# Pooled attention scores on the four free tiles of TensorE's array, between the local scores

## Chip, core and metric

The kernel runs on one core of one Trainium2 chip. The metric is the device time of one execution in microseconds; the time before is the median of three runs. A core has five engines with queues of their own: TensorE (PE in the profile, with PEld for its weight loads), VectorE (DVE), ScalarE (ACT), GpSimd (POOL) and SyncE (SP), which only issues transfers.

## The reference

An attention with two branches, added, and a gated feed-forward network behind it.

```python
# q, k, v: 8 batches x 8 heads x 576 x 64
q_d = q.reshape(B, H, Sd, factor, D).mean(axis=3)      # factor 4, Sd = 144; k_d, v_d alike
out_d = sm_attn(q_d, k_d, v_d)                         # softmax attention on the pooled sequence
out_up = np.repeat(out_d, factor, axis=2)
mask = np.abs(pos[:, None] - pos[None, :]) < factor    # local branch: 7 keys for each query
scores = np.where(mask, scale * np.matmul(q, k.transpose(0, 1, 3, 2)), -1000000000.0)
out_local = np.matmul(softmax(scores), v)
x = (out_up + out_local).transpose(0, 2, 1, 3).reshape(B * S, H * D)     # 4608 x 512
gate = np.maximum(x @ w_gate, 0.0)                     # 512 x 1536
return (gate * (x @ w_val) @ w_out).astype(np.float32) # 1536 x 512
```

## The kernel before

Two heads of one batch are a pair p, so there are 32 pairs. `pair(p)` builds the steps of one: loading and casting q and k, transposing them (on TensorE for p < 8, by a DMA after that), pooling (`pl`, the reduction at L1507 on VectorE for p >= 4), the scores, both softmaxes, and the products with v, which `xa` adds into the transposed input xT of the network. `first` builds the two first products of the network (L1794) with their ReLU and product on ScalarE and VectorE (L1808, L1815), `second` the last product (L1860) and the output. A planner (`list_schedule`) gives every step a time on its engine from durations and ranks that are written into the kernel, and the program issues them in that order: on each engine the order is fixed, and only semaphores hold an instruction back.

The scores are one TensorE step `S{p}` for p >= 4 (28 steps), made by `emit_S` from `emit_Sl` and then `emit_Sd`, in two PSUM banks. For the first four pairs (`hd`) `Sl{p}` and `Sd{p}` are steps of their own. The two heads lie in the two halves of the partitions, so each matmul takes 64 rows of the array (row half hh). The output is in groups of 32 partitions, and a matmul with 32 weight columns takes one column group c of four. The array is thus used as eight tiles, 2 row halves x 4 column groups.

- *Local scores* (L1519): 12 rounds of four matmuls, each 32 queries against 32 keys. Round i has blocks 2i and 2i + 1 (par = 0, 1) for both heads, on tiles (hh, c = 2 par + hh): (0,0), (1,1), (0,2), (1,3).
- *Pooled scores* (L1538): 3 rounds of four matmuls, 32 pooled queries against all 144 pooled keys, on tiles (hh, c = 2 hh + par): (0,0), (1,2), (0,1), (1,3). They read qkd, which `pl` writes.

Below, L0 to L11 are the local rounds and P0 to P2 the pooled ones. VectorE adds the mask to the local scores (`msk`, L1576) and takes the pooled scores' maximum (`dmx`, L1588); ScalarE takes the pooled exponentials from the other bank (L1601). The pooled weights wd are turned round by TensorE and evicted by `evw` for p < 8, and by a DMA for the others; `wcols(hh, kc)` picks a head's columns of the result, wT, for the product with the pooled v (L1735).

Of the kernel before, what the change touches and what calls it, by code (L numbers as in the profile page):

```python
# [1192 lines left out]
def _sap(t_ap, lo, n, extra_off, free_dims):  # L1193
    pitch = t_ap.ap[0][0]
    return bass.AP(
        tensor=t_ap.tensor,
        offset=t_ap.offset + lo * pitch + extra_off,
        ap=[[pitch, n]] + [list(d) for d in free_dims],
    )
# [22 lines left out]
def kernel(  # L1222
# [10 lines left out]
    nc = tc.nc  # L1233
    B, H, S, D = q.shape
    NP = B * H // 2
    SD = S // 4
# [35 lines left out]
    def many(n, shape, dt, name):  # L1272
        return [pool.tile(shape, dt, name=f"{name}{i}") for i in range(n)]
# [9 lines left out]
    mask_sb = pool.tile([128, 12, 32], BF16, name="mask_sb")  # L1283
    ident = pool.tile([128, 128], FP16, name="ident_sb")
# [11 lines left out]
    wT = many(3, [128, 6, 128], FP16, "wT")  # L1296
    tq = many(3, [128, 9, 128], FP16, "tq")
    sums_sb = pool.tile([128, 256], FP16, name="sums_sb")
    qkd = many(3, [128, 2 * SD], FP16, "qkd")
# [9 lines left out]
    bank = [psum.tile([128, 512], FP32, name=f"bank{i}") for i in range(8)]  # L1309
# [3 lines left out]
    def add(*a, **kw):  # L1313
        o = Op(*a, **kw)
        ops.append(o)
        return o
# [9 lines left out]
    def copies(dst, src, *engines):  # L1326
        def on(eng):
            if eng == ACT:
                return lambda o: nc.scalar.copy(out=dst, in_=src(o))  # L1329
            return lambda o: engine[eng].tensor_copy(out=dst, in_=src(o))  # L1330
        return [(e, d, on(e)) for e, d in engines]

    def add_any(forms, deps, **kw):

        kw.setdefault("bias", 0.8 if kw["prio"] < 200.0 else BIAS)
        return add(*forms[0], deps, alts=forms[1:], **kw)

    def half(i):
        return bank[i].bitcast(FP16)
# [58 lines left out]
    def pair(p):  # L1398
        b, kk = p // 4, p % 4
        base = 2 * p * HS  # L1400
        S4, S3, S2 = p % 4, p % 3, p % 2
# [3 lines left out]
        hd = p < HEAD  # L1405
# [15 lines left out]
        g = p // 2  # L1421
# [43 lines left out]
        step, q0, k0 = (1, 0, S) if p < TD else (2, QK0, QK0 + 1)  # L1465
        qk_sums = _sap(qk_, 0, 128, q0, [[k0 - q0, 2], [4 * step, SD], [step, 4]])

        def cols(hh, t0, n):
            return _sap(qk_, 64 * hh, 64, t0, [[step, n]])

        old_qk = [b3.get("S"), b3.get("pl"), z_qk[S3]]
        if p < TD:
# [4 lines left out]
            for i, t0, nt in ((0, 0, nb0), (1, nb0, tk - nb0)):  # L1477
# [3 lines left out]
                    lambda o, i=i, nt=nt: _sap(half(T.banks[i]), 0, 128, 0,  # L1481
                                               [[1, 2], [2, nj], [n2, nt]]),
# [27 lines left out]
            pl = add(DVE, 1.35, emit_pool, [*evs, b3.get("S")], prio=P + 14, name=f"pl{p}")  # L1510
        r["pl"] = pl

        def local_scores(scv):
            for i in range(12):
                for par in range(2):
                    blk = 2 * i + par
                    for hh in range(2):
                        c = 2 * par + hh
                        nc.tensor.matmul(  # L1519
                            out=scv[32 * c : 32 * c + 32, i, :],  # L1520
                            lhsT=cols(hh, q0 + step * 24 * blk, 32),
                            rhs=cols(hh, k0 + step * (24 * blk - 3), 32),
                            start=not hd, stop=not hd or i == 11)

        def emit_Sl(o):
            if hd:
                nc.tensor.matmul(out=bank[o.banks[0]][:, 0:384], lhsT=ident, rhs=mask_sb,
                                 start=True, stop=False)
            local_scores(bank[o.banks[0]][:, 0:384].rearrange("p (i j) -> p i j", j=32))

        def emit_Sd(o):
            spv = bank[o.banks[-1]][:, 0 : 3 * SD].rearrange("p (i j) -> p i j", j=SD)
            for i in range(3):
                for par in range(2):
                    g = 2 * i + par
                    for hh in range(2):
                        c = 2 * hh + par
                        nc.tensor.matmul(  # L1538
                            out=spv[32 * c : 32 * c + 32, i, :],
                            lhsT=qkd[S3][64 * hh : 64 * hh + 64, 24 * g : 24 * g + 32],  # L1540
                            rhs=qkd[S3][64 * hh : 64 * hh + 64, SD : 2 * SD],
                            start=True, stop=True)

        def emit_S(o):
            emit_Sl(o)
            emit_Sd(o)
        if hd:
            Sx = add(PE, 0.65, emit_Sl, [*evs, ld_mask], prio=P + 20, need=(pool_, 1),
                     key=("S", p), name=f"Sl{p}", n=49)
            r["S"] = Sd = add(PE, 0.45, emit_Sd, [pl, Sx], prio=P + 20.5, need=(pool_, 1),  # L1550
                              key=("Sd", p), name=f"Sd{p}", n=12)
        else:
            r["S"] = Sx = Sd = add(PE, 0.67, emit_S, [*evs, pl], prio=P + 20, need=(pool_, 2),
                                   key=("S", p), name=f"S{p}", n=60, bias=MARGIN)
        kd = Sd.key

        def lview():
            return bank[Sx.banks[0]][:, 0:384].rearrange("p (i j) -> p i j", j=32)

        def dview():  # L1560
            return bank[Sd.banks[-1]][:, 0 : 3 * SD].rearrange("p (i j) -> p i j", j=SD)
# [3 lines left out]
        def bc12(t):  # L1565
            return _sap(t, 0, 128, 0, [[1, 12], [0, 32]])

        if hd:
            mxo = add(DVE, 0.55, lambda o: nc.vector.tensor_reduce(
                out=mx[S3], in_=lview(), axis=AX.X, op=ALU.max), [Sx, z_w], prio=P + 23,  # L1570
                name=f"mx{p}")
            sub = add(DVE, 0.56, lambda o: nc.vector.tensor_tensor(
                out=s_, in0=lview(), in1=bc12(mx[S3]), op=ALU.subtract),
                [mxo, b2.get("exp")], prio=P + 24, free=[("S", p)], name=f"sub{p}")
        else:
            msk = add(DVE, 0.56, lambda o: nc.vector.tensor_tensor(  # L1576
                out=s_, in0=lview(), in1=mask_sb, op=ALU.add),
                [Sx, ld_mask, b2.get("exp")], prio=P + 21, free=[("S", p)], name=f"msk{p}")
            mxo = add(DVE, 0.55, lambda o: nc.vector.tensor_reduce(  # L1579
                out=mx[S3], in_=s_, axis=AX.X, op=ALU.max), [msk, z_w], prio=P + 23,  # L1580
                name=f"mx{p}")
            sub = add_any(either(lambda o, e: e.tensor_tensor(  # L1582
                out=s_, in0=s_, in1=bc12(mx[S3]), op=ALU.subtract), (POOL, 0.84), (DVE, 0.56)),
                [mxo], prio=P + 24, name=f"sub{p}", port=(DVE, POOL))
        r["exp"] = ex = add(ACT, 0.53, lambda o: nc.scalar.activation(
            out=e_, in_=s_, func=AF.Exp, scale=scale),
            [sub, b3.get("tr0"), b3.get("tr1")], prio=P + 25, name=f"exp{p}")
        dmax = add(DVE, 0.60, lambda o: nc.vector.tensor_reduce(  # L1588
            out=nmx[S3][:, 0:3], in_=dview(), axis=AX.X, op=ALU.max,
            negate=True), [Sd, b3.get("nrd")], prio=P + 22, name=f"dmx{p}")  # L1590
        nb = add(POOL, 0.23, lambda o: nc.gpsimd.tensor_scalar(  # L1591
            out=nmb[S3][:, 0:3], in0=nmx[S3][:, 0:3], scalar1=scale / 16.0, scalar2=None,
# [3 lines left out]
        K0, KR = (0, 96) if p < VPOOL else (V0, V0 + 72)  # L1596
# [3 lines left out]
        for i in range(3):  # L1600
            exd.append(add(ACT, 0.37, lambda o, i=i: nc.scalar.activation(  # L1601
                out=_sap(wd_, 0, 128, 256 * i + K0, kd_cols),
# [5 lines left out]
            out=sm[S3], in_=e_, axis=AX.X, op=ALU.add), [ex, warm], prio=P + 26, name=f"sm{p}")  # L1608
# [3 lines left out]
            out=e_, in0=e_, in1=bc12(rs[S3]), op=ALU.mult), (POOL, 0.84), (DVE, 0.5)),  # L1612
            [rco], prio=P + 28, name=f"nrm{p}", port=(DVE, POOL))
        tr = []
        for par in range(2):
            lo = 64 * par
            tr.append(add(DVE, 0.575, lambda o, lo=lo: nc.vector.transpose(  # L1617
                out=at2[S3][lo : lo + 64, :, lo // 2 : lo // 2 + 32],
# [5 lines left out]
            out=rsd[S3].rearrange("p (i k) -> p i k", k=2),  # L1624
# [3 lines left out]
            out=_sap(wd_, 0, 128, K0, w3), in0=_sap(wd_, 0, 128, K0, w3),  # L1628
# [9 lines left out]
        if p < TD:  # L1638
            r["W"] = W = add(PE, 0.34, emit_W, [nrd], prio=P + 30, need=(pool_, 1),
                             key=("W", p), name=f"W{p}", n=6)  # L1640

            evw = add_any(copies(
                _sap(wT[S3], 0, KR, 0, [[48, 6], [2 * SD, 2], [24, 2], [1, 24]]),
                lambda o: _sap(half(W.banks[0]), 0, KR, 0,
                               [[128, 6], [64, 2], [32, 2], [1, 24]]),
                (ACT, 0.64), (DVE, 0.74)),
                [W, b3.get("V")], prio=P + 31, free=[("W", p)], name=f"evw{p}")
            wcols = lambda hh, kc: _sap(wT[S3], 0, KR, (2 * hh + kc) * SD, [[1, SD]])
        else:
            r["W"] = evw = add(SP, 1.5, lambda o: nc.sync.dma_start(  # L1650
                wT[S3], _sap(wd_, 0, 128, 0, [[1, 768]]), transpose=True),
                [nrd, b3.get("V")], prio=P + 30, xfer=0.8, name=f"dW{p}")
            wcols = lambda hh, kc: _sap(wT[S3], 0, KR, 128 * kc + 64 * hh,
                                        [[256, 3], [32, 2], [1, 24]])
        r["evw"] = evw


# [3 lines left out]
        for par in range(2):  # L1661
            for hh in range(2):
                c = 2 * par + hh
# [38 lines left out]
        else:  # L1702
# [8 lines left out]
            else:  # L1711
                l4 = b1["l4"]
            r["vs"] = vso = add_any(either(lambda o, e: e.tensor_tensor(  # L1713
                out=vs[0], in0=v4_[:, :, 0:128], in1=v4_[:, :, 128:256], op=ALU.add),
# [4 lines left out]
                out=vdz4, in0=vs4[:, :, :, 0:64], in1=vs4[:, :, :, 64:128], op=ALU.add),  # L1719
# [5 lines left out]
        def emit_V(o):  # L1725
# [21 lines left out]
            out=od_sb[S2], in_=bank[V.banks[0]][:, 288 : 288 + SD], mul=0.25),  # L1747
# [212 lines left out]
```

## Time and profile before

| | |
|---|---|
| time, median of 3 runs (lowest to highest) | 364.08 us (363.34 to 364.46) |
| the profiled execution: its span, from the first to the last instruction | 365.8 us |
| mean clock granted to TensorE | 0.991 |
| local score matmuls, L1519: number, busy, mean | 1536, 16.9 us, 177 ns |
| pooled score matmuls, L1538: number, busy, mean | 384, 12.0 us, 225 ns |

The span is taken from one profiled execution; its own time is that span, 0.5% over the median of the runs, which were taken without a profile. Times in the profile are in us unless marked ns. A matmul's record has a start and a modelled end; matmuls overlap, so busy times of TensorE are not added up from means. In a row of busy time by stretch, each engine has its busy time and, behind an x, how many of its instructions ran in the stretch; then come TensorE's granted clock, the share of the DMA engines, and GB/s. In a row of waits stand the waiting engine with its line, what released it, the time in all, how often, and the longest.

### The profile page before, as it was taken

What the parts mean: (1) busy time and instruction counts of PE and PEld (TensorE: products, weight loads), DVE (VectorE), ACT (ScalarE), POOL (GpSimd) and SP (SyncE); (2) the same over time, 40 slices, a digit from 0 to 9 for tenths busy, and PEclk for the clock granted to TensorE, in tenths of its full rate; (3) what the DMA queues carried; (4) which work ended last, traced back from release to release, by engine and by line L of the source; (5) the groups of instructions that cost most, each with busy time, mean ns of one, the idle gap of its engine ahead of it and who ended that gap; (6) DMA issues with size and microseconds to landing.
All of it is one profiled execution on the core that took longest, in us unless ns stands there. A gap on an engine that the chain in (4) does not pass through costs nothing.

```text
span 365.8 us, 10503 instructions
## 1 busy us (share of the span) xinstructions
PE 354.5 (97%) x4241; PEld 183.5 (50%) x4241; DVE 248.5 (68%) x477; ACT 203.0 (55%) x481; POOL 204.7 (56%) x240
## 2 busy tenths in 40 slices
PE   8869999999999999999999999999999999999996
PEld 3536556445554554545454445544545554445554
DVE  4557789726889698887895986788988853322210
ACT  2356977536875667556566675768565433223222
POOL 7677575861557979675888458585799400000000
PEclk9979999999999999999999999999999999999999
DMA  7999999489999999999999999999996121011012
GB/s 189 161 246 274 196 222 300 82 150 192 235 233 219 257 263 148 250 200 273 230 182 238 185 293 160 200 269 211 229 236 109 25 80 57 0 59 57 1 68 107
DMA packets 122067, 64.80 MB, mean 177 GB/s; under 512 B 100386, under 2 KB 106402, under 8 KB 122018
## 3 DMA queue, kind: packets, MB, share of 16 engines
q1 hardware_dynamic: 116194, 59.41, 75.2%
q0 software_dynamic: 5824, 4.72, 8.4%
q8 instruction: 33, 0.54, 0.6%
q14 instruction: 16, 0.13, 0.1%
HBM read 47.59 MB, written 9.44 MB: 156 GB/s over the span
## 4 chain that ended last, share of the span: by engine, by line
PE 90%; DMA 4%; DVE 2%; SPq 1%; POOL 1%; issue 1%; ACT 1%; POOLq 0%
PE bank L1794 52%; PE bank L1860 25%; PE bank L1519 4%; PE bank L1727 2%; DMA gT<-in_k_dram 2%; PE bank L1735 2%; DMA mask_sb<-band_mask 2%; PE bank L1538 2%; PE bank L1636 1%; PE bank L1691 1%; PE bank L1456 1%; DVE vw L1352 1%; PE bank L1839 1%; SPq L1430 1%; SPq L1676 1%
## 5 line engine op out<-in xcount | busy, mean ns | idle before, releaser
L1815 DVE TENSOR_TENSOR gT<-r,bank 128x512 f16<-128x512 f16 (+1 forms) x112 | 74.6, 667 | 64.3 <-PE bank L1794 61.2
L1794 PE MATMUL bank<-xT,wv_sb 128*128 128x512 f16 (+2 forms) x528 | 112.4, 341 | 0.1
L1794 PE MATMUL bank<-xT,wg_sb 128*128 128x512 f16 (+2 forms) x528 | 112.2, 341 | 0.0
L1808 ACT ACTIVATE r<-bank 128x512 f16<-128x512 f32 (+1 forms) x112 | 65.1, 582 | 70.0 <-PE bank L1794 62.9
L1860 PE MATMUL bank<-wo_sb,gT 128*128 128x512 f16 x420 | 96.6, 379 | 0.0
L1794 PEld LDWEIGHTS <-wg_sb 128*128 128x128 f16 x528 | 44.2, 98 | 46.5 <-issue 0.6
L1794 PEld LDWEIGHTS <-wv_sb 128*128 128x128 f16 x528 | 44.2, 98 | 45.5 <-issue 1.0
L1860 PEld LDWEIGHTS <-gT 128*128 128x128 f16 x420 | 39.8, 98 | 45.2 <-issue 0.4
L1869 ACT COPY y_sb<-bank 128x512 f32<-128x512 f32 x35 | 20.5, 586 | 51.5 <-PE bank L1860 51.5
L1330 POOL CAST vw<-vw 128x1536 f16<-128x1536 f32 x28 | 40.9, 1462 | 4.0 <-PE bank L1860 2.3
L1507 DVE TENSOR_REDUCE qkd<-qkT 128x288 f16<-128x1152 f16 x28 | 37.6, 1342 | 3.5 <-ACT qkT L1329 3.1
L1601 ACT ACTIVATE wd<-bank,nmb 128x144 f16<-128x144 f32 x96 | 35.6, 380 | 6.3 <-POOL nmb L1591 5.5
L1582 POOL TENSOR_TENSOR s_sb<-s_sb,mx 128x384 f32<-128x384 f32 x28 | 23.3, 832 | 27.0 <-DVE mx L1579 26.8
L1617 DVE STREAM_TRANSPOSE at<-e 64x384 f16<-64x384 f16 x64 | 36.4, 569 | 2.0 <-POOL e L1611 1.3
L1611 POOL TENSOR_TENSOR e<-e,rs 128x384 f16<-128x384 f16 x32 | 26.8, 839 | 15.1 <-DVE rs L1609 11.8
L1627 POOL TENSOR_TENSOR wd<-wd,rsd 128x432 f16<-128x432 f16 x32 | 29.0, 909 | 9.3 <-DVE rsd L1623 7.6
L1755 DVE TENSOR_TENSOR xT<-bank,od_sb 128x288 f16<-128x288 f32 (+2 forms) x68 | 26.7, 431 | 10.0 <-ACT od_sb L1746 9.8
L1329 ACT COPY qkT<-tq 128x1152 f16<-128x1152 f16 x21 | 25.3, 1204 | 3.0 <-DMA tq<-c 3.0
L1713 POOL TENSOR_TENSOR vs<-v 104x512 f32<-104x512 f32 x20 | 25.4, 1269 | 0.9 <-DMA v<-in_v_dram 0.6
L1330 POOL CAST c<-qk 128x1152 f16<-128x1152 f32 x16 | 18.2, 1147 | 5.5 <-issue 3.2
L1588 DVE TENSOR_REDUCE nmx<-bank 128x3 f32<-128x432 f32 x32 | 19.0, 594 | 3.2 <-PE bank L1538 3.1
L1519 PEld LDWEIGHTS <-qkT 64*32 64x32 f16 x1536 | 13.8, 90 | 12.9 <-issue 7.2
(67 smaller groups left out, 349.9 us busy)
## 6 DMA issues: line engine op xcount, KB each, us to landing
vw<-in_v_dram SPq DMA_DIRECT2D x126, 96.0 KB, 4.8
out_dram<-y_sb SPq DMA_DIRECT2D x16, 512.0 KB, 3.4
qk<-in_q_dram SPq DMA_DIRECT2D x14, 576.0 KB, 6.7
qk<-in_k_dram SPq DMA_DIRECT2D x14, 576.0 KB, 6.4
v<-in_v_dram SPq DMA_DIRECT2D x10, 640.0 KB, 6.5
wv_sb<-in_moe_w_val_dram POOLq DMA_DIRECT2D x4, 384.0 KB, 9.3
wg_sb<-in_moe_w_gate_dram POOLq DMA_DIRECT2D x4, 384.0 KB, 9.4
wo_sb<-in_moe_w_out_dram POOLq DMA_DIRECT2D x4, 384.0 KB, 7.2
```

The source lines that it names most:

```text
L1330: return lambda o: engine[eng].tensor_copy(out=dst, in_=src(o))
L1507: nc.vector.tensor_reduce(out=qkd[S3].rearrange("p (x t) -> p x t", x=2), in_=qk_sums, axis=AX.X, op=ALU.add)
L1519: nc.tensor.matmul(out=scv[32 * c : 32 * c + 32, i, :], lhsT=cols(hh, q0 + step * 24 * blk, 32), rhs=cols(hh, k0 + step * (24 * blk - 3), 32),
L1601: exd.append(add(ACT, 0.37, lambda o, i=i: nc.scalar.activation(out=_sap(wd_, 0, 128, 256 * i + K0, kd_cols), in_=_sap(dview()[:, i, :], 0 ...
L1611: r["nrm"] = nrm = add_any(either(lambda o, e: e.tensor_tensor(out=e_, in0=e_, in1=bc12(rs[S3]), op=ALU.mult), (POOL, 0.84), (DVE, 0.5)), ...
L1617: tr.append(add(DVE, 0.575, lambda o, lo=lo: nc.vector.transpose(out=at2[S3][lo : lo + 64, :, lo // 2 : lo // 2 + 32], in_=e_[lo : lo + 64 ...
L1627: r["nrd"] = nrd = add_any(either(lambda o, e: e.tensor_tensor(out=_sap(wd_, 0, 128, K0, w3), in0=_sap(wd_, 0, 128, K0, w3), in1=_sap(rsd[ ...
L1755: nc.vector.tensor_tensor(out=xT[:, kk, (c1 + lo) % XR : (c1 + lo) % XR + hi - lo].rearrange("p (t f) -> p t f", f=4), in0=bank[V.banks[hf ...
L1794: nc.tensor.matmul(out=bank[(h or o).banks[0]][:, n * x : n * x + n], lhsT=w_sb[:, kk, bass.ts(jj, 128)], rhs=xT[:, kk, x_col(t0) : x_col( ...
L1808: rl = add(ACT, 0.17 + 0.00083 * n * m, lambda o: nc.scalar.activation(out=rt[:, 0 : n * m], in_=bank[f1.banks[0]][:, 0 : n * m], func=AF. ...
L1815: gm = add(DVE, 0.15 + 0.00104 * n * m, lambda o: nc.vector.tensor_tensor(out=gT[:, js[0] : js[0] + m, pos : pos + n], in0=rt[:, 0 : n * m ...
L1860: nc.tensor.matmul(out=bank[parts[0].banks[0]], lhsT=gT[:, jj, col : col + 128], rhs=wo_sb[:, jj, :], start=(jj == 0), stop=(jj == NJJ - 1))
```

## The change

The local and the pooled loops become functions of one round, `local_round` and `pooled_round`. `emit_S` issues a pooled round behind local rounds 0, 2 and 4. The pooled matmuls move to other column groups: c = 2 par + 1 - hh, that is tiles (0,1), (1,0), (0,3), (1,2), the four that a local round leaves free. With that the 32-partition groups of the pooled scores hold other head and block combinations, so `evw` reads them in another order and `wcols` takes other columns. The steps, their durations in the planner, and the order of steps on every engine stay.

```diff
-        def local_scores(scv):
+        def local_round(scv, i):
+            for par in range(2):
+                blk = 2 * i + par
+                for hh in range(2):
+                    c = 2 * par + hh
...
+        def pooled_round(spv, i):
+            for par in range(2):
+                g = 2 * i + par
+                for hh in range(2):
+                    c = 2 * par + 1 - hh
+                    nc.tensor.matmul(
+                        out=spv[32 * c : 32 * c + 32, i, :],
+                        lhsT=qkd[S3][64 * hh : 64 * hh + 64, 24 * g : 24 * g + 32],
+                        rhs=qkd[S3][64 * hh : 64 * hh + 64, SD : 2 * SD],
+                        start=True, stop=True)
...
         def emit_Sd(o):
-            spv = bank[o.banks[-1]][:, 0 : 3 * SD].rearrange("p (i j) -> p i j", j=SD)
             for i in range(3):
-                for par in range(2):
-                    g = 2 * i + par
-                    for hh in range(2):
-                        c = 2 * hh + par
...
+                pooled_round(dview(), i)
 
         def emit_S(o):
-            emit_Sl(o)
-            emit_Sd(o)
+            for i in range(12):
+                local_round(lview(), i)
+                if i % 2 == 0 and i < 6:
+                    pooled_round(dview(), i // 2)
...
-                               [[128, 6], [64, 2], [32, 2], [1, 24]]),
+                               [[128, 6], [32, 2], [64, 2], [1, 24]]),
...
-            wcols = lambda hh, kc: _sap(wT[S3], 0, KR, (2 * hh + kc) * SD, [[1, SD]])
+            wcols = lambda hh, kc: _sap(wT[S3], 0, KR, (2 * (1 - hh) + kc) * SD, [[1, SD]])
...
-            wcols = lambda hh, kc: _sap(wT[S3], 0, KR, 128 * kc + 64 * hh,
-                                        [[256, 3], [32, 2], [1, 24]])
+            wcols = lambda hh, kc: _sap(wT[S3], 0, KR, 128 * kc + 32 * (1 - hh),
+                                        [[256, 3], [64, 2], [1, 24]])
```

TensorE, the first merged step: qkT2 holds its q and k, qkd2 the pooled ones, bank4 takes local scores and bank6 pooled ones. Before, at the end of the local rounds:

```order
L1519 LDWEIGHTS qkT2_116
L1519 MATMUL bank4_142<-qkT2_116 32x32
L1538 LDWEIGHTS qkd2_111
L1538 MATMUL bank6_144<-qkd2_111 32x144 [waits DVE_49]
L1538 LDWEIGHTS qkd2_111
L1538 MATMUL bank6_144<-qkd2_111 32x144
```

and with the change, at the end of the first local round:

```order
L1518 LDWEIGHTS qkT2_116
L1518 MATMUL bank4_142<-qkT2_116 32x32
L1530 LDWEIGHTS qkd2_111
L1530 MATMUL bank6_144<-qkd2_111 32x144 [waits DVE_49]
L1530 LDWEIGHTS qkd2_111
L1530 MATMUL bank6_144<-qkd2_111 32x144
```

The first pooled pair, with its wait for VectorE, stood behind 48 local pairs and stands behind four; the last local pair, which stood ahead of 12 pooled ones, now ends the step.

VectorE, around the scores of two pairs (s_sb is the masked local scores, nmx the pooled maximum). Before:

```order
L1576 TENSOR_TENSOR s_sb_90<-bank_144,mask_sb 128x384 [waits PE_49]
L1579 TENSOR_REDUCE mx_119<-s_sb_90 128x12 [waits DVE_49]
L1588 TENSOR_REDUCE nmx_128<-bank_142 128x3 [waits PE_49]
L1815 TENSOR_TENSOR gT<-r_78,bank_138 128x512 [waits PE_49,Activation_49]
L1507 TENSOR_REDUCE qkd_109<-qkT_114 128x288 [waits Activation_49]
```

and with the change:

```order
L1580 TENSOR_TENSOR s_sb_90<-bank_144,mask_sb 128x384 [waits PE_49]
L1583 TENSOR_REDUCE mx_119<-s_sb_90 128x12 [waits DVE_49]
L1592 TENSOR_REDUCE nmx_128<-bank_142 128x3
L1819 TENSOR_TENSOR gT<-r_78,bank_138 128x512 [waits PE_49,Activation_49]
L1507 TENSOR_REDUCE qkd_109<-qkT_114 128x288 [waits Activation_49]
```

No instruction moved. The pooled maximum needs no wait of its own any more where the masking ahead of it has waited for the later local matmuls. Where the maximum stands first it is the other way round, and the masking has a wait that it had not.

More of the change, by code (lines that the diff above doesn't have):

```diff
@@ L1511, in pair @@
         r["pl"] = pl
-        def local_scores(scv):
-            for i in range(12):
-                for par in range(2):
-                    blk = 2 * i + par
-                    for hh in range(2):
[L1518 to L1529, printed above, removed]
+        def local_round(scv, i):
[4 more added lines that the diff above has]
+                    nc.tensor.matmul(
+                        out=scv[32 * c : 32 * c + 32, i, :],
+                        lhsT=cols(hh, q0 + step * 24 * blk, 32),
+                        rhs=cols(hh, k0 + step * (24 * blk - 3), 32),
+                        start=not hd, stop=not hd or i == 11)
@@ new lines, in pooled_round, with emit_Sl @@
+        def pooled_round(spv, i):
[3 more added lines that the diff above has]
+                    c = 2 * par + 1 - hh
+                    nc.tensor.matmul(
+                        out=spv[32 * c : 32 * c + 32, i, :],
+                        lhsT=qkd[S3][64 * hh : 64 * hh + 64, 24 * g : 24 * g + 32],
+                        rhs=qkd[S3][64 * hh : 64 * hh + 64, SD : 2 * SD],
+                        start=True, stop=True)
+        def emit_Sl(o):
+            nc.tensor.matmul(out=bank[o.banks[0]][:, 0:384], lhsT=ident, rhs=mask_sb,
+                             start=True, stop=False)
+            for i in range(12):
+                local_round(lview(), i)
@@ L1531, in emit_Sd @@
         def emit_Sd(o):
-            spv = bank[o.banks[-1]][:, 0 : 3 * SD].rearrange("p (i j) -> p i j", j=SD)
             for i in range(3):
-                for par in range(2):
-                    g = 2 * i + par
-                    for hh in range(2):
-                        c = 2 * hh + par
[L1538 to L1542, printed above, removed]
+                pooled_round(dview(), i)
@@ L1544, in emit_S @@
         def emit_S(o):
-            emit_Sl(o)
-            emit_Sd(o)
+            for i in range(12):
+                local_round(lview(), i)
+                if i % 2 == 0 and i < 6:
+                    pooled_round(dview(), i // 2)
         if hd:
```

## The prediction

> **What bounds the kernel now.** I read the busy table first, then the chain that ended last, and then went down to one score step.
>
> ```profile
> span 365.8 us, 10503 instructions
> PE 354.5 (97%) x4241; PEld 183.5 (50%) x4241; DVE 248.5 (68%) x477; ACT 203.0 (55%) x481; POOL 204.7 (56%) x240
> PE 90%; DMA 4%; DVE 2%; SPq 1%; POOL 1%; issue 1%; ACT 1%; POOLq 0%
> ```
>
> TensorE (PE) is busy for 97% of the span, and 90% of the chain of waits runs through it. The waits between 41 and 284 us, where all 28 score steps with a merged body (S4 to S31) lie, say the same:
>
> ```profile
> PE bank L1519 <- DVE xT L1755: 0.7, 1, 0.7
> PE bank L1519 <- issue: 0.4, 1, 0.4
> ```
>
> These two rows are all that TensorE waited for in 243 us. So time taken out of a TensorE step there reaches the end of the kernel, as long as no other engine becomes the later one.
>
> **One score step as it is.** The timeline around the step at 93.5 us, first three rows (start, duration, engine, line), and the forms of the two groups over the whole run (minimum, median, maximum in ns):
>
> ```profile
> 93.50 0.53 PE L1519 MATMUL bank<-qkT 64*32 64x32 f16 x48
> 93.85 0.38 PE L1538 MATMUL bank<-qkd 64*32 64x144 f16 x12
> 94.16 0.82 PE L1794 MATMUL bank<-xT,wg_sb 128*128 128x512 f16 x3
> L1519 PE MATMUL bank<-qkT x1536: 173/173/189, 12.4 to 283.6; 64*32 64x32 f16 x192
> L1538 PE MATMUL bank<-qkd x384: 219/223/233, 12.7 to 283.8; 64*32 64x144 f16 x192
> ```
>
> The step owns TensorE from 93.50 to 94.16, which is 0.66 us: 0.35 us in which the 48 local matmuls are started, then 0.31 us for the 12 pooled ones until the next step's first matmul. The chain has the last step of this kind with the same length, 284.01 - 283.35 = 0.66:
>
> ```profile
> 283.35 0.46 PE bank L1519 x48
> 284.01 6.15 PE bank L1794 x28
> ```
>
> How fast the matmuls start is read from stretches with one beginning and growing ends; the first x is how many matmuls had started by then. First the local ones, then the pooled ones of the same step:
>
> ```profile
> 93.45:93.54 0.09, 0.04 (x4) 0.04 (x8) 1.00 1.11 77
> 93.45:93.60 0.15, 0.10 (x14) 0.10 (x18) 1.00 0.77 77
> 93.45:93.72 0.27, 0.22 (x33) 0.22 (x33) 1.00 0.45 51
> 93.45:93.85 0.40, 0.35 (x48) 0.35 (x48) 1.00 0.38 46
> 93.45:93.85 0.40, 0.00 (x0) 0.00 (x1) 1.00 0.38 46
> 93.45:93.89 0.44, 0.04 (x4) 0.04 (x6) 1.00 0.34 42
> 93.45:93.95 0.50, 0.10 (x8) 0.10 (x12) 1.00 0.33 46
> 93.45:94.01 0.56, 0.16 (x12) 0.16 (x12) 1.00 0.34 62
> ```
>
> Two paces are to be seen. 33 matmuls start in the first 0.22 us, some 6.5 ns each, or 25 ns per round of four. The remaining 15 take from 93.72 to about 93.85, some 8.4 ns each. The slower pace begins 0.22 us in, 0.03 us after the first matmul has ended (189 ns at most). My reading: about 32 weight-load and matmul pairs lie ready in TensorE's queue when the step begins, a place becomes free when a matmul ends, and from then on pairs come in at 8.4 ns. The pooled rounds start some 0.06 us apart, slower than pairs come in: 144 columns set them.
>
> **The change, part by part.** Nothing is added or removed: 60 matmuls and 60 weight loads per step stay, with their shapes. Three things move.
>
> *First, the pooled rounds go between the local ones.* The new order is L0 P0 L1 L2 P1 L3 L4 P2 and then L5 to L11. The first eight rounds are just the 32 pairs that lie ready. If a pooled round runs beside the local ones on its own four tiles, eight rounds start in about 0.22 us, as eight local rounds do now. Then the queue decides. The 33rd pair follows at 0.22. The 37th needs the place of the fifth, and that is now P0's first matmul: it starts at about 0.04 (the row x4 by 93.54), lasts 0.223 to 0.233, and 0.03 passes until its place is filled: 0.04 + 0.23 + 0.03 = 0.30. From the 37th to the 60th it is 23 x 8.4 ns = 0.19, so the last local matmul starts at 0.49 us.
>
> *Second, the step ends with a 32-column matmul and not with a 144-column one.* How long the array needs before the next step can load weights is read from the same place and from the one head step in which local matmuls stand alone:
>
> ```profile
> 94.16 0.55 PEld L1794 LDWEIGHTS <-wg_sb 128*128 128x128 f16 x4
> 19.91 0.53 PE L1519 MATMUL bank<-qkT 64*32 64x32 f16 x48 [0.21 <-ACT qkT L1329]
> 20.37 0.17 PEld L1691 LDWEIGHTS <-sums_sb 128*32 128x32 f16 x6
> ```
>
> After pooled matmuls: the last started by 94.01, the next load came at 94.16, 0.15 us later. After local ones: the last started at 19.91 + 0.53 - 0.18 = 20.26, the next load came at 20.37, 0.11 us later. So the step will be 0.49 + 0.11 = 0.60 us instead of 0.66: 0.06 us less, and 28 x 0.06 = 1.7 us in all. This is what I take.
>
> The ends of this term: if places are given back without waiting for P0, the last pair starts at 0.22 + 27 x 8.4 ns = 0.45, the step takes 0.56, and 28 x 0.10 = 2.8 us go. If a pooled round holds up its local neighbours for its full 0.06 us, the last starts at 0.50 to 0.54 and 0.01 to 0.05 us a step go, 0.3 to 1.4 us. Below nothing: rival C. I stay between them: no row of before has a short matmul behind a long one inside a step, and the nearest, the 33rd start 0.03 us after the first end, fits a queue whose oldest place comes free first, so P0's place must come before L1's. The Trainium skill, "TensorE: Matmul & The Clock Gate", Part 3 (The mechanism), says that matmuls start and end strictly in program order; by that P0 holds back what is behind it and the step is 0.60, while without it the step would be 0.56. No run here shows order of ends inside one step, since their ends are modelled.
>
> *Third, readiness.* Local scores are finished at 0.49 + 0.18 = 0.67 us into the step, where it was 0.35 + 0.18 = 0.53; pooled ones at about 0.19 + 0.23 = 0.42, where it was 0.51 + 0.22 = 0.73. VectorE (DVE) reads both:
>
> ```profile
> DVE gT L1815 <- PE bank L1794: 22.5, 33, 4.9
> DVE nmx L1588 <- PE bank L1538: 3.1, 6, 1.4
> DVE s_sb L1576 <- PE bank L1519: 2.6, 4, 1.4
> 220.00:284.00 64.00, 64.00 (x858) 32.41 (x856) 53.72 (x102) 40.88 (x96) 49.32 (x56) 1.00 1.06 201
> ```
>
> In those 243 us only 4 of its local reads and 6 of its pooled ones waited at all. Four times 0.14 us later against six times 0.3 us earlier costs nothing; were it not so, 4 x 0.14 = 0.6 us of VectorE time would be lost, and VectorE has 22.5 us in that stretch in which it waits for TensorE anyway. In the densest stage it is busy for 53.7 of 64 us. The pooled matmuls' wait for the reduction L1507 moves up from 0.35 us to 0.04 us into the step, and all local rounds but the first now queue behind it. No step of TensorE waited for L1507 in the rows above, so I price that at nothing; a reduction that came 0.3 us late would now cost up to its lateness, once per step concerned.
>
> The eviction evw reads the same values in another order, and the columns that L1735 streams come in pieces of 24 at a new distance. Both at nothing: the 80 matmuls whose columns come in pieces and the 48 of which 32 stream whole rows have one mean today,
>
> ```profile
> L1735 PE MATMUL bank<-wT,vdz 104*128 104x144 f16 x80 | 8.2, 224 | 0.0
> L1735 PE MATMUL bank<-wT,vdz 96*128 96x144 f16 x48 | 4.9, 224 | 0.0
> ```
>
> and only the first eight pairs take the eviction. The head steps keep their separate local and pooled blocks.
>
> **Sum.** 365.8 us (the profiled execution, 0.5% over the median of the runs, 364.08) less 1.7 is 364.1; in the median's terms 364.08 - 1.7 = 362.4 us.
>
> **Rivals.**
>
> A: *the step shrinks fully* (0.56 us, places free without regard to P0). For it: free tiles, other banks, and the last 28 pairs at 8.4 ns need nothing else. Against: the 33rd pair's wait. 364.1 - 2.8 = 361.3 us.
>
> B: *pooled and local rounds take turns*, since now two halves of the array feed the same 32 output partitions at one time, and no matmuls in the trace before do that: the present local rounds lie on a diagonal. Then the step takes 0.61 to 0.65 and the kernel 362.7 to 363.8. The Trainium skill, "TensorEngine Tiling (Array Packing)", Restrictions and Gotchas, says that different row tiles write to different PSUM banks and cannot use one bank at the same time. Local and pooled scores go to two banks, so by that page turns are not needed between them; yet it would forbid today's local round, whose two row halves write one bank and whose four matmuls start in 25 ns, so here the trace does not agree with it.
>
> C: *slower*. Each change of row half inside a column group empties the pipe first. The price of emptying is in the tails above: 0.11 us less some 0.01 us for streaming 32 columns (112 more cost 0.04) is about 0.1 us. There would be six such changes in a step, from L0 to P0, back, and so on: +0.6 us, of which some 0.1 is absorbed by the queue's wait; 0.5 x 28 = 13 us, 377 us. It decides from about 17 ns per change, where 6 x 17 = 0.10 us eats the whole gain of the full overlap. Against it: at 93.85 the pooled round follows the last local one, on tiles of which two share a column group with the other half, and its four matmuls all start within 0.04 us; no gap of 0.1 is seen. For it: that place shows the change once, not with long and short matmuls side by side.
>
> D: *the change does what it says and the end stays*: another engine or the DMA engines, whose share is 1.06 in the last stage quoted, take over the bound. Against it are the 22.5 us that VectorE waits for TensorE, and that TensorE waits for no DMA after 41 us. 364.0 us.
>
> **Chances.** The forecast (0.60 us a step, 361.9 to 362.9 us) 0.42; A 0.20; B 0.13; D 0.10; C 0.15. A measurement of this kernel can tell about 0.3% (1.1 us) from no change, so faster is below 363.0: nearly all of the forecast (0.41), A (0.20) and a third of B (0.05), 0.66. Within 0.3%: the rest of B (0.08), D (0.09) and a little of the forecast (0.01), 0.18. Slower: C and 0.01 of D, 0.16. The range reaches from A's lower end, 361.0, to just above no change, 364.4; C is left out.
>
> **What would show it.** Right: the merged steps are 0.60 us from first local matmul to the next step's first; pooled matmuls start inside the first 0.2 us; the pause stands after the 36th pair, at 0.25 to 0.30 us; the next weight load follows the last local matmul by 0.11 us; TensorE's waits stay near 1 us. A is right if there is no pause and the step is 0.56. B shows as local rounds that start 0.06 us after each pooled one, C as gaps near 0.1 us, D as steps of 0.60 with new rows in TensorE's waits. I am wrong if the step is over 0.66 us.

## The result, and the profile after

| | before | with the change |
|---|---|---|
| median of 16 runs each (lowest to highest), us | 364.35 (363.34 to 367.82) | 361.92 (361.35 to 364.82) |
| ratio to before, 95% interval | 1 | 0.9942 (0.9923 to 0.9962) |
| span of the profiled execution, us | 365.8 | 359.6 |

The change is 0.6% faster: 0.58% of 364.35 is 2.1 us, and by the interval 1.4 to 2.8. 362.4 had been predicted, with a range of 361.0 to 364.4. The two spans differ by more, 6.2 us, but 3.8 of that lies ahead of the first merged step, which starts at 41.58 us in the one profile and at 37.79 in the other though the order up to there is the same. That stretch differs from one execution to the next: the seven timed experiments below have the first merged step between 38.1 and 41.9. It goes with the clock granted to TensorE, the third number from the end in these two rows of before, which is 1.00 in both for the changed kernel:

```profile
20.00:25.00 5.00, 3.05 (x75) 1.17 (x75) 3.07 (x8) 2.05 (x8) 2.61 (x3) 0.70 1.26 240
25.00:30.00 5.00, 4.31 (x43) 3.45 (x43) 1.34 (x3) 3.27 (x11) 5.00 (x7) 0.61 1.07 309
```

The experiment with 41.9 (e6) has 0.94 and 0.50 there. A run's time is 1.7 to 1.9 us longer than its span wherever both are on record, so the profiled execution of before, with its span of 365.8, took some 367.6 us by this estimate, 1% over the median and not 0.5%. From here on only what follows the first merged step is compared.

The page of the changed kernel, its span, busy times and chain by engine:

```profile
span 359.6 us, 10503 instructions
PE 350.2 (97%) x4241; PEld 182.5 (51%) x4241; DVE 247.9 (69%) x477; ACT 202.8 (56%) x481; POOL 204.5 (57%) x240
PE 90%; POOL 5%; DMA 1%; issue 1%; DVE 1%; ACT 1%; POOLq 0%; SPq 0%
```

TensorE is the bound as before. One merged step, on the timeline (start, duration, engine, line; L1518 is now the local matmul, L1530 the pooled one):

```profile
89.34 0.20 PE L1518 MATMUL bank<-qkT 64*32 64x32 f16 x4
89.35 0.24 PE L1530 MATMUL bank<-qkd 64*32 64x144 f16 x4
89.38 0.21 PE L1518 MATMUL bank<-qkT 64*32 64x32 f16 x8
...
89.49 0.23 PE L1530 MATMUL bank<-qkd 64*32 64x144 f16 x4
89.56 0.44 PE L1518 MATMUL bank<-qkT 64*32 64x32 f16 x28
89.92 1.04 PE L1798 MATMUL bank<-xT,wg_sb 128*128 128x512 f16 x4
```

The first pooled round starts 0.01 us behind the first local one, and the local rounds L1 and L2 start inside its 0.06 us. The step is 89.92 - 89.34 = 0.58 us, where it was 0.66. By the starts of its matmuls, 26 of the 28 steps take 582 to 585 ns (median 0.583 us). The local matmuls of the same step again in stretches with one beginning, the first x being those started by then:

```profile
89.30:89.47 0.17, 0.13 (x20) 0.13 (x21) 1.00 0.51 81
89.30:89.56 0.26, 0.22 (x21) 0.22 (x21) 1.00 0.55 106
89.30:89.60 0.30, 0.26 (x24) 0.26 (x25) 1.00 0.50 100
89.30:89.62 0.32, 0.28 (x25) 0.28 (x26) 1.00 0.49 101
89.30:89.81 0.51, 0.47 (x48) 0.47 (x48) 1.00 0.56 136
```

L0 to L4 have started by 89.47. No further local matmul comes until 89.56, where the 33rd pair of the step, L5's first, starts 0.22 us in. Then there is a second pause: L5's four have started by 89.60, and by 89.62 a single one of L6 has followed. That one is the 37th pair; it starts 0.274 us in, 0.033 behind the 36th, where the pairs around it are 8 ns apart. This is the pause that the forecast asked for.

The first merged step (that of pair 5) did not gain. First before, then with the change:

```profile
41.58 0.52 PE L1519 MATMUL bank<-qkT 64*32 64x32 f16 x48 [0.66 <-DVE xT L1755]
41.94 0.37 PE L1538 MATMUL bank<-qkd 64*32 64x144 f16 x12
42.24 0.39 PE L1794 MATMUL bank<-xT,wg_sb 128*128 128x512 f16 x1
...
37.79 0.20 PE L1518 MATMUL bank<-qkT 64*32 64x32 f16 x4 [0.66 <-DVE xT L1759]
38.15 0.24 PE L1530 MATMUL bank<-qkd 64*32 64x144 f16 x4 [0.17 <-DVE xT L1759]
38.72 0.39 PE L1798 MATMUL bank<-xT,wg_sb 128*128 128x512 f16 x1
```

Its pooled part waits 0.36 us for a bank that VectorE's addition into xT (L1759) frees, and 44 local matmuls wait behind it: 0.93 us, where before the pooled part started as late, but behind 48 local matmuls that were running meanwhile, and the step was 0.66.

TensorE's waits after 37 us are the two from this step and no others; of VectorE's waits three rows answer to those shown of before:

```profile
PE bank L1518 <- DVE xT L1759: 0.7, 1, 0.7
PE bank L1530 <- DVE xT L1759: 0.2, 1, 0.2
DVE gT L1819 <- PE bank L1798: 21.3, 33, 4.9
DVE s_sb L1580 <- PE bank L1518: 3.1, 4, 1.6
DVE nmx L1592 <- PE bank L1530: 1.3, 2, 1.0
```

The pooled maximum waits twice instead of six times, and the masking as often as before for 0.5 us more.

So much of the gain is accounted for: 26 x 0.077 = 2.0 us from the steps, less 0.26 in the first. The fourth merged step has a stall in both kernels in which TensorE waits for nothing that the profile shows; it is 1.18 us long before and 0.81 after, but 1.12 and 1.34 in two repeats of the changed kernel, so its difference is not the change's. That leaves 1.7 us, inside the measured 1.4 to 2.8. The two profiles differ by 2.4 us from the first merged step on; beside the 0.37 of that stall there are 0.3 us outside the steps, which one profile of each kernel cannot put down to the change.

### The profile page after: what moved, and what is told of

It reads as the page before. It is cut to its first block, busy times and chain, and to the rows that moved or that the text cites. A ratio compares the mean times of both kernels' runs of the same rounds, so it can differ in the third digit from the quotient of the medians.

```text
span 359.6 us, 10503 instructions
## 1 busy us (share of the span) xinstructions
PE 350.2 (97%) x4241; PEld 182.5 (51%) x4241; DVE 247.9 (69%) x477; ACT 202.8 (56%) x481; POOL 204.5 (57%) x240
## 4 chain that ended last, share of the span: by engine, by line
PE 90%; POOL 5%; DMA 1%; issue 1%; DVE 1%; ACT 1%; POOLq 0%; SPq 0%
PE bank L1798 52%; PE bank L1864 25%; PE bank L1518 4%; PE bank L1731 2%; PE bank L1739 2%; DMA gT<-in_q_dram 1%; PE bank L1530 1%; POOL wo_sb L1330 1%; PE bank L1640 1%; PE bank L1695 1%; POOL vw L1352 1%; POOL wd L1631 1%; PE bank L1843 1%; POOL vw L1330 1%; POOL e L1615 1%
## 5 line engine op out<-in xcount | busy, mean ns | idle before, releaser
L1507 DVE TENSOR_REDUCE qkd<-qkT 128x288 f16<-128x1152 f16 x28 | 37.5, 1340 | 3.7 <-ACT qkT L1329 3.5
L1759 DVE TENSOR_TENSOR xT<-bank,od_sb 128x288 f16<-128x288 f32 (+2 forms) x68 | 26.7, 430 | 9.9 <-ACT od_sb L1750 9.8
L1518 PEld LDWEIGHTS <-qkT 64*32 64x32 f16 x1536 | 17.2, 90 | 11.9 <-issue 7.3
L1518 PE MATMUL bank<-qkT 64*32 64x32 f16 x1536 | 20.6, 180 | 1.0 <-DVE xT L1759 0.7
```

The lines of the kernel that those rows point to most:

```text
L1507: nc.vector.tensor_reduce(out=qkd[S3].rearrange("p (x t) -> p x t", x=2), in_=qk_sums, axis=AX.X, op=ALU.add)
L1518: nc.tensor.matmul(out=scv[32 * c : 32 * c + 32, i, :], lhsT=cols(hh, q0 + step * 24 * blk, 32), rhs=cols(hh, k0 + step * (24 * blk - 3), 32),
L1759: nc.vector.tensor_tensor(out=xT[:, kk, (c1 + lo) % XR : (c1 + lo) % XR + hi - lo].rearrange("p (t f) -> p t f", f=4), in0=bank[V.banks[hf ...
```

## The experiments

The theory (Q) is that of the prediction: some 32 pairs lie ready in TensorE's queue, a place comes free when the oldest matmul ends, pairs then follow at 8.4 ns, and a short last matmul lets the next step load 0.04 us earlier. The rival (F) puts the gain to the free tiles alone: what counts is that pooled and local matmuls run side by side.

**e1, the change once more.** No edit.

> The changed kernel once more, beside the others on one chip. Theory Q (the queue): places in TensorE's queue come free in the order of the matmuls' ends, about 32 pairs lie ready, pairs follow at 8.4 ns, and 0.11 us pass after the last local matmul. By it a merged step is 0.58 us as in the profile after, and the time is 0.6% under the kernel before. Rival F (the free tiles): what counts is only that pooled and local matmuls run side by side on tiles of their own; the same number here.

Steps of 0.583 us; ratio 0.9951 (0.9931 to 0.9971). It is the mark for the others of its chip.

**e2, the order of the change on the old tiles.**

```diff
-                    c = 2 * par + 1 - hh
+                    c = 2 * hh + par
```

with `evw` and `wcols` as before the change.

> The order of the change, but the pooled matmuls on the tiles that they had before (c = 2 hh + par), two of which a local round uses too. Theory Q: local rounds behind a pooled one now wait for its 0.06 us, L5 starts at 0.33 us instead of 0.22, but the queue lets the 49th pair in only at 0.40 and the last local matmul starts at 0.49: a step of 0.60 us, 28 x 0.06 = 1.6 us under before, ratio about 0.9955. Rival F: without free tiles nothing runs side by side, a step is 0.66 us as before, ratio 1.000.

```profile
90.31 0.20 PE L1518 MATMUL bank<-qkT 64*32 64x32 f16 x4
90.33 0.24 PE L1530 MATMUL bank<-qkd 64*32 64x144 f16 x3
...
90.61 0.38 PE L1518 MATMUL bank<-qkT 64*32 64x32 f16 x26
90.92 1.04 PE L1798 MATMUL bank<-xT,wg_sb 128*128 128x512 f16 x4
```

The step is 0.61 us (median 0.608), ratio 0.9963 (0.9942 to 0.9984), and the last local matmul starts at 0.493. F's 0.66 did not come. L5 can't be told by name here, since rounds no longer start together: 22 local matmuls have started by 0.25 us, the other 26 start from 0.29 on. Seven of these stand 25 ns apart, the pace of one tile, from 0.325 to 0.476. If they are L5 to L11 on a shared tile, L5 begins 0.33 us in, as worked out; but then a shared tile by itself ends the step within 0.02 us of where the queue ends it. So e2 does not test the queue. Nor is it without free tiles: of the old ones (0,1) and (1,2) are free in a local round, and the first pooled matmuls start 0.02 us in. Of the 0.077 us that the change takes from a step, the new order brings some 0.05 with two of the four tiles free, and freeing the other two brings 0.025 on top of it. Free tiles in the old order were not tried.

**e3, pooled rounds late.**

```diff
-                if i % 2 == 0 and i < 6:
-                    pooled_round(dview(), i // 2)
+                if 7 <= i < 10:
+                    pooled_round(dview(), i - 7)
```

> The new tiles, pooled rounds behind local rounds 7, 8 and 9 instead of 0, 2 and 4, so that all 32 pairs that lie ready are local. Theory Q: no long matmul holds back a place, all 28 later pairs follow at 8.4 ns, the last local matmul starts at 0.45 us, a step is 0.56 us, 0.02 less than the change: 0.6 us in 28 steps, and some 0.2 us more in the first merged step, whose pooled part waits for its bank with 32 local matmuls ahead of it again. Ratio to before 0.992. Rival F: the same three pooled rounds run beside local ones, a step stays 0.58 us, ratio 0.994.

```profile
90.35 0.37 PE L1518 MATMUL bank<-qkT 64*32 64x32 f16 x32
90.56 0.26 PE L1530 MATMUL bank<-qkd 64*32 64x144 f16 x4
...
90.91 1.04 PE L1798 MATMUL bank<-xT,wg_sb 128*128 128x512 f16 x4
```

0.56 us a step (median 0.559), and 0.66 in the first merged one: Q again. No pause is left behind the 33rd pair. But the time did not follow, ratio 0.9964 (0.9941 to 0.9987). In the profile 305.5 us lie outside the 28 steps (from the first one's start to the end, less all their lengths), 305.0 in e1. Against e1, matmul by matmul, this run is 0.65 us ahead at 246.6 us and loses 0.40 at the next matmul (0.25 had been lost at 135.8 us), where ScalarE waited for a transfer of k and was late with the ReLU that frees TensorE's bank:

```profile
245.53 1.15 ACT L1329 CAST c<-qk 128x1152 f16<-128x1152 f32 x1 [1.50 <-DMA qk<-in_k_dram]
```

A further 0.2 us goes in the 26th merged step, which takes 0.75 us. The pooling reduction ends 0.40 us after the step has begun, and the pooled matmuls start 0.45 us in, where 0.21 is usual:

```profile
262.54 1.31 DVE L1507 TENSOR_REDUCE qkd<-qkT 128x288 f16<-128x1152 f16 x1
263.45 0.37 PE L1518 MATMUL bank<-qkT 64*32 64x32 f16 x32
263.90 0.24 PE L1530 MATMUL bank<-qkd 64*32 64x144 f16 x4
```

The same step has a late reduction in e5, e6 and e8 below and takes 0.69, 0.78 and 1.05 us. The reduction ended 0.07 us ahead of it before, and 0.58 ahead of it in the profile of the change.

**e4, pooled rounds first.**

```diff
+            for i in range(3):
+                pooled_round(dview(), i)
             for i in range(12):
                 local_round(lview(), i)
-                if i % 2 == 0 and i < 6:
-                    pooled_round(dview(), i // 2)
```

> The new tiles, all three pooled rounds ahead of the local ones. Theory Q: they are the first 12 of the 32 ready pairs, end at 0.23, 0.30 and 0.36 us, and hold back the 33rd, 37th and 41st pair to 0.26, 0.33 and 0.39 us; the last local matmul starts at 0.55 us and a step is 0.66 us: no gain, ratio 1.000, though the step ends with a short matmul and two pooled rounds overlap nothing. Rival F: local rounds begin beside the third pooled one, at 0.15 us, and the step is 0.15 + 0.35 + 0.11 = 0.61 us or less, ratio 0.996 or less.

Local matmuls started by a growing end in a step that begins at 97.535 us; then the step's first rows on the timeline, and the next step's first:

```profile
97.50:97.72 0.22, 0.15 (x20) 0.15 (x21) 1.00 0.58 27
97.50:97.79 0.29, 0.22 (x20) 0.21 (x21) 1.00 0.46 24
97.50:97.83 0.33, 0.26 (x24) 0.24 (x25) 1.00 0.41 23
97.50:97.85 0.35, 0.28 (x24) 0.26 (x25) 1.00 0.40 23
97.50:97.91 0.41, 0.34 (x28) 0.32 (x29) 1.00 0.35 22
97.53 0.24 PE L1530 MATMUL bank<-qkd 64*32 64x144 f16 x4
97.57 0.20 PE L1518 MATMUL bank<-qkT 64*32 64x32 f16 x4
97.61 0.23 PE L1530 MATMUL bank<-qkd 64*32 64x144 f16 x2
...
98.20 0.29 PE L1798 MATMUL bank<-xT,wv_sb 128*128 128x64 f16 x4
```

There are three pauses, ahead of the 33rd, 37th and 41st pair (the 21st, 25th and 29th local one), which start 0.261, 0.323 and 0.386 us in; 0.26, 0.33 and 0.39 had been expected. Each ends some 0.03 us after the first matmul of one pooled round has ended. The step is 0.66 us (median 0.663) and the ratio 0.9992 (0.9970 to 1.0015): the overlap and the short last matmul are there, and the gain is gone. That is Q, and F's 0.61 is out. In ten of its 28 steps the 45th pair came 0.027 us later still and the step took 0.69; why is open.

One thing here neither theory had. All 12 pooled matmuls stand ahead of the local ones in the program, yet the first four local ones start 0.04 us in and the second pooled round, whose tiles are still busy, only at 0.07. So matmuls on tiles of their own do not start in program order. Places nevertheless come free in program order: L0 ends at 0.04 + 0.19 = 0.23, but the 37th pair waits for the fifth, the first of P1, which ends at 0.295.

**e5, pooled rounds behind 9, 10 and 11**, so that the step ends with a pooled round.

```diff
-                if i % 2 == 0 and i < 6:
-                    pooled_round(dview(), i // 2)
+                if i >= 9:
+                    pooled_round(dview(), i - 9)
```

> The new tiles, pooled rounds behind local rounds 9, 10 and 11, so that the step ends with a 144-column matmul again. Theory Q: all pairs behind the 32nd follow at 8.4 ns, the last pooled matmul starts at 0.45 us, and 0.15 us pass behind it instead of 0.11: a step of 0.60 us, 0.04 us longer than with pooled rounds behind 7, 8 and 9, ratio about 0.9955. Rival F: three pooled rounds run beside local ones as in the change, 0.58 us, ratio 0.994.

```profile
90.12 0.46 PE L1518 MATMUL bank<-qkT 64*32 64x32 f16 x40
...
90.54 0.25 PE L1530 MATMUL bank<-qkd 64*32 64x144 f16 x4
90.72 1.04 PE L1798 MATMUL bank<-xT,wg_sb 128*128 128x512 f16 x4
```

0.60 us, 0.04 more than e3, where the same pooled rounds come two local rounds earlier; ratio 0.9955 (0.9920 to 0.9989), too wide to be told from the change.

**e6 and e7, late rounds and the change again**, on one chip.

> Pooled rounds behind 7, 8 and 9 once more, beside the change on one chip. Steps of 0.56 us again. If the queue's gain of 0.02 us a step and of 0.26 us in the first merged step reaches the end, the time is 0.8 us under the change, ratio to before about 0.992; if what TensorE gains is given back at a late transfer, as ScalarE's 1.5 us wait for k at 245 us in the first profile of it suggests, the time is that of the change, 0.9945.

> The change beside the late rounds on one chip: steps of 0.58 us, ratio to before 0.9945 in either case.

Late rounds 0.9956 (0.9923 to 0.9989), the change 0.9944 (0.9913 to 0.9975), with steps of 0.556 and 0.583 us. The intervals overlap, so neither is shown to be better; twice the late rounds brought some 0.025 us less per step and not less time. The profiled execution of e6 has a wait that the change's have not, 0.8 us for the turned weights:

```profile
PE bank L1739 <- DMA wT<-wd: 0.8, 1, 0.8
```

and 306.6 us outside the steps, against 305.4 in e7. But that execution took 366.7 us, 2.3 us over e6's median, so this wait does not explain the median.

**e8 and e9, one step alone with late rounds**, one execution each.

```diff
-                if i % 2 == 0 and i < 6:
+                if p == HEAD and 7 <= i < 10:
+                    pooled_round(dview(), i - 7)
+                if p != HEAD and i % 2 == 0 and i < 6:
```

> The change, but the first merged step alone with its pooled rounds behind 7, 8 and 9. If its 0.93 us come from the pooled matmuls' wait for their bank, which the masked and added output of the first pair frees late, that step is 0.66 us as before, with all others at 0.58; if the step is long for another reason (instructions not yet loaded), it stays at 0.93.

The edit took the wrong step: the first merged step in the program is pair 5's, and pair 4's, the second, became 0.56 us while the first stayed at 0.93. It showed something else. In the 26th step, at 263 us, the pooled part waited for the pooling reduction:

```profile
262.95 0.20 PE L1518 MATMUL bank<-qkT 64*32 64x32 f16 x4
263.44 0.24 PE L1530 MATMUL bank<-qkd 64*32 64x144 f16 x4 [0.29 <-DVE qkd L1507]
264.00 0.39 PE L1866 MATMUL bank<-wo_sb,gT 128*128 128x512 f16 x1
```

That step took 1.05 us. e9 has `p == 5` and `p != 5` in the place of the two conditions:

> The experiment e8 changed pair 4, but the first merged step in the program's order is that of pair 5. Here pair 5 alone has its pooled rounds behind 7, 8 and 9. If its 0.93 us come from the pooled matmuls' wait for their bank, the first merged step is 0.66 us, all others 0.58; if they come from elsewhere, it stays at 0.93.

```profile
37.97 0.37 PE L1518 MATMUL bank<-qkT 64*32 64x32 f16 x32 [0.66 <-DVE xT L1761]
38.34 0.24 PE L1530 MATMUL bank<-qkd 64*32 64x144 f16 x4
38.64 0.39 PE L1800 MATMUL bank<-xT,wg_sb 128*128 128x512 f16 x1
```

0.67 us: the pooled matmuls still start 0.37 us in, when their bank is free, but 32 local ones have started meanwhile. The 0.93 us of the change come from that wait. Another step of e9, with early pooled rounds, waited 0.6 us for the reduction and took 1.40 us.

## Why the prediction was right, point by point

- *TensorE bounds, so a shorter step reaches the end.* Right for the change: 304.9 us lie outside its 28 steps from the first of them to the end, 305.2 before.
- *The order of the first 32 pairs, then the 33rd at 0.22 us.* Right, 0.216.
- *The 37th pair waits for P0's first matmul.* The mechanism was right, and e4, in which three pooled rounds give three pauses, is its test. One premise was not: e4 shows that matmuls need not start in program order; it is the places that come free in that order. The size of the term was off: P0 was put at 0.04 us, where a second local round starts; on free tiles it started at 0.013, so the 37th pair came at 0.27 and not 0.30, and the last local matmul at 0.47 and not 0.49.
- *0.11 us behind a short last matmul.* Right: 0.114. With e5 against e3 it is 0.04 us of the step by itself.
- *The step: 0.60 us.* It is 0.583, so the gain of a step was 0.077 and not 0.06, for the reason just named. The sum was 1.7 us; with the measured step and the loss below it is again 1.7. That is luck: steps that gained more than forecast and a loss that was not forecast cancel.
- *The pooled wait moved up, at nothing.* This step failed. The prediction asked only whether TensorE had waited for the reduction L1507, and overlooked that the pooled matmuls also wait for their bank. That wait was there before too, hidden behind the local rounds of its own step, so no row of waits showed it: 0.26 us in the first merged step. The lateness of the reduction, which the prediction did name, cost something in e3, e5, e6, e8 and e9, most where the pooled rounds stand early: 0.47 us in e8 for 0.43 us late, 0.2 in e3 for 0.40.
- *Readiness for VectorE, at nothing.* Right on the whole: 1.8 us less of waiting for pooled scores, 0.5 more for local ones.
- *The eviction and the cut columns, at nothing.* Right: the product's mean is the same 224 ns, and the eviction's 636 ns where it was 635.

```profile
L1739 PE MATMUL bank<-wT,vdz 104*128 104x144 f16 x80 | 8.2, 224 | 0.0
L1329 ACT COPY wT<-bank 96x576 f16<-96x576 f16 x8 | 5.1, 636 | 2.2 <-PE bank L1640 2.1
```

Of the rivals, A (full shrinking) is out, since the pause is there; where it can be had, in e3 and e6, the step is 0.56 as A said. B is out for the change: L1 starts 27 ns behind P0, though pooled rounds on the same tiles stand some 60 ns apart. e2, where two of the four tiles are shared, took 0.61, the lower end of B. C is out, no gap of 0.1 us stands at a change of row half (and its sum was short: 0.5 x 28 is 14 us, not 13). D did not decide the change, but e3 is what it described: shorter steps, and waits elsewhere that take them back. That those waits come from TensorE's lead is not shown. The late reduction of e3 stands in e8 too, whose steps but one are those of the change, and in both ScalarE had just waited for a transposed transfer (tq), 2.1 and 2.2 us, where it waited 1.0 in the profile of the change.

## What to carry to other kernels

In a burst of small matmuls, count in pairs of load and matmul and ask which pair waits for which place in the queue: a long matmul at the head of the burst delays the pair 32 places behind it, so the shortest step has the long ones behind the first 32 pairs and not at the end, where they lengthen the pause before the next kind of work. Here that made the step shorter than the change's, but not the kernel. Here the order, tried first and with two of the four tiles free, was the larger part of the gain of a step, and the other two free tiles the smaller. Before a wait is moved ahead of other work, look for every condition on the instruction, its output's bank too, since a wait that is hidden today stands in no row.

## What the hardware showed that had not been expected

- A pooled matmul (144 columns) and local ones (32 columns) on the other row half of the same column group run side by side here, where they write different banks: P0 to P2 start 13, 87 and 149 ns into the step, with local rounds at 0, 40, 67, 92 and 117 ns between them.
- Rounds on free tiles need not keep the 25 ns that local rounds keep on their own tiles: 13 ns lie between L0 and P0, and 5 between P1 and L3.
- A local matmul on a free tile starts ahead of a pooled one that stands before it in the program and waits for its tile: 0.04 against 0.07 us in e4.
- The pause between the end of a matmul, as the profile models it, and the start of the pair that takes its place was 28 ns in the change, where P0's first matmul ends at 13 + 233 ns and the 37th pair starts at 274, and the same to 1 ns in the three pauses of e4.
